# Loading the block-sum input of an attention kernel as one transfer of 128 rows, or as four of 24 rows, one per head

## The chip, the cores and the metric

The kernel runs on one core of a Trainium2 chip. The metric is the device time of one execution in microseconds (us); lower is better. Six names recur: PE is TensorE (matmuls, and PEld its weight loads), DVE is VectorE, ACT is ScalarE, POOL is GpSimd, and SP is the engine that here only issues transfers. "SPq" in a profile line is SP's stream of transfer issues, "POOLq" that of POOL.

## The reference

The inputs are q, k and v of shape (4, 8, 768, 64) in float32, and the weights of a small mixture of attention experts. Cut to what matters:

```
# stage 1, per batch b and head h (S = 768, D = 64, 24 blocks of 32 tokens)
k_sum = k.reshape(B, H, 24, 32, D).max(axis=3)
v_sum = v.reshape(B, H, 24, 32, D).mean(axis=3)
scores_all = concat([where(|i - j| < 16, scale * q @ k.T, -1e9),
                     scale * q @ k_sum.T + log(32)])
x = softmax(scores_all) @ concat([v, v_sum])
# stage 2, per batch: x (768 x 512) goes through 4 causal attention experts (64 wide),
# each token's output is the softmax-weighted sum over its two best experts
```

The change is about how v is brought in for `v_sum`, the mean of v over each block of 32 tokens.

## The kernel before, in words

Batches b run over 0 to 3. In stage 1 the 8 heads of a batch are taken as 4 pairs c; two pairs make a group g of 4 heads. Nothing is scheduled at run time. Every piece of work is a named step, and a table written out by hand (`TABLE`) lists all steps in one order, each with the engine that runs it and the buffer slots that it takes. Each engine executes its own steps strictly in that order, so a step that waits holds everything behind it on its engine. The names used below are a step's kind, then b, then c or g, then a part.

The steps that touch the change:

- `dvs`b g (L373, L376) is issued by SP. It loads the v of 4 heads into the buffer `vt` (128 partitions of 2048 float32). Partition 32*j + n holds block n of head j: 32 tokens of 64 values, 8 KB, contiguous in memory. The rows 24 to 31 of each head's 32 partitions are not used by anything later. `vt` has one slot only, so each load waits until the additions on the one before it have read it.
- `tr`b g 0 and 1 (L384) are the additions on POOL that fold 2048 values to 64, in five instructions (1024, 512, 256, 128, 64 wide) over partitions 0 to 119. The last writes `vu`.
- `ds`b c (L181 on POOL or DVE, L179 on ACT) copies the sums from `vu` into rows 96 to 119 of the value buffer `vb`, twelve times over.
- `dv`b c (L312) is SP's load of v for the window, in rows of 256 bytes, into `vb`.
- `av`b c u (L478 on PE) multiplies the softmax weights by `vb`; it needs both `dv` and `ds`.

This tree of loads and additions is used for the groups (1,1), (2,0), (2,1), (3,0) and (3,1); the others sum v by matmuls (L337).

Around them: `dk` and `dq` (L289) are the loads of k and q, issued by POOL, in POOL's order between the additions; `tk` (L409) and `tq` (L435) are the transposes on PE that need them; `pp` (L653), `vp` (L585, L588), `sp` (L677), `es` (L685 on ACT), `dm` (L690 on POOL), `aw` (L701), `tw` (L737) and `op` (L755) are stage 2 of the previous batch; `od` (L766) is SP's store of the output; L503 is a transpose on PE of the stage 1 result.

SP's order around the loads is: dwv, **dvs11**, dv12, dwo, dv13, **dvs20**, dv21, dv20, **dvs30**, dv23, **dvs21**, od02, dv22, od00, **dvs31**, od01, dv30, dv32. In POOL's order, dk200 and dk210 stand ahead of tr200; dq300, dk310, dq210 and dk300 stand between tr201 and tr300; tr310 follows on tr211 and a copy.

A step of kind `dvs` starts after `vt` was set to zero once, at the beginning (`vtz`, L278).

Of the kernel before, what the change touches and what calls it, by code (L numbers as in the profile page):

```python
# [13 lines left out]
B = 4  # L14
H = 8
S = 768
D = 64
# [5 lines left out]
NSUM = 24  # L23
# [146 lines left out]
def make_plan(nc, T, q, k, v, moe_w_gate, moe_wq, moe_wk, moe_wv, moe_wo, out):  # L170
# [3 lines left out]
    def en(e):  # L174
        return getattr(nc, ENG[e])

    def copy(e, dst, src):
        if e == "A":
            nc.scalar.copy(dst, src)  # L179
        else:  # L180
            en(e).tensor_copy(dst, src)  # L181
# [185 lines left out]
    def tree(b, g):  # L367
        t, u = R.buf("vt"), R.buf("vu")

        def load(e):  # L370
            x, vh = T["vt"][t.slot], v[b, 4 * g]
            full = 4 if (b, g) != (B - 1, 1) else 3
            nc.sync.dma_start(out=x[0:32 * full, :],  # L373
                              in_=bass.AP(vh.tensor, vh.offset, [[S * D, full], [32 * D, 32], [1, 32 * D]]))
            if full == 3:
                nc.sync.dma_start(out=x[96:96 + NSUM, :],  # L376
                                  in_=bass.AP(vh.tensor, vh.offset + 3 * S * D, [[32 * D, NSUM], [1, 32 * D]]))
        R.step(f"dvs{b}{g}", {"S": 1.8}, [vtz], [t], load, dma=3.0)
        for i, ws in enumerate(((1024,), (512, 256, 128, 64))):
            def add(e, ws=ws):  # L380
                x = T["vt"][t.slot]
                for w in ws:
                    y = T["vu"][u.slot] if w == 64 else x[:, 0:w]
                    en(e).tensor_tensor(y[0:120], x[0:120, 0:w], x[0:120, w:2 * w], AL.add)  # L384
            R.step(f"tr{b}{g}{i}", {"G": sum(0.13 + w * 0.00218 for w in ws)}, [t],
                   [u] if i else [t], add, keep=[t])
        for c in (2 * g, 2 * g + 1):
            def dsum(e, c=c):
                for h in range(2):
                    j = 32 * (2 * (c % 2) + h)  # L390
                    copy(e, T["vb"][vb[b, c].slot][WIN:KR, 12 * h + 1:12 * h + 13, 0:64],
                         T["vu"][u.slot][j:j + NSUM, :].unsqueeze(1).to_broadcast((NSUM, NQ, 64)))
            R.step(f"ds{b}{c}", {"G": 1.75, "V": 0.95, "A": 1.64}, [u], [vb[b, c]], dsum)
# [517 lines left out]
```

## Time and profile before

| what | value |
|---|---|
| median of 3 runs | 227.06 us (222.6 to 229.35) |
| the profiled execution's own time | 223.95 us |
| its span, first to last instruction | 222.2 us |
| mean granted TensorE clock | 0.879 of full speed |
| busy PE, DVE, ACT, POOL | 159.6, 136.2, 125.4, 91.7 us |
| additions on `vt` (L384), mean of one of the 20 that write `vt` | 1200 ns |
| POOL's wait for `vt` from memory | 41.5 us in 4 waits |
| moved by transfers | 28.27 MB |

The profile is one execution. Its instructions are shown by engine with their line in the kernel, and idle time is put down to what ended it. The time of an execution is 1.75 us above the span in the profiled run. "DMA share" is the mean busy share of the core's 16 transfer engines.

### The profile page before, as it was taken

The page shows a single profiled execution, that of the slowest core. Times are in us where ns is not written, and L with a number is a line of the kernel's source. Part 1 is how long each engine was busy: PE and PEld are TensorE (multiplying, and loading weights), DVE is VectorE, ACT ScalarE, POOL GpSimd, SP SyncE. Part 2 cuts the span into 40 slices and gives each one's busy share as a digit, 9 for nine tenths or more (in the row PEclk, how much of TensorE's full clock was granted, in tenths as well). Part 3 has the DMA queues.
Part 4 walks back from the last instruction along what each step waited for, and adds up shares of the span by engine and source line. Part 5 has one row for each costly group of instructions (what it writes and reads, how often), then busy time and mean ns, then how long its engine had stood idle before and what let it go on. Part 6 is the DMA issues. An engine that isn't in the chain of part 4 may idle for free.

```text
span 222.2 us, 6444 instructions
## 1 busy us (share of the span) xinstructions
PE 159.6 (72%) x2796; PEld 119.2 (54%) x2796; DVE 136.2 (61%) x251; ACT 125.4 (56%) x158; POOL 91.7 (41%) x149
## 2 busy tenths in 40 slices
PE   0283986599689964989504994399509999999860
PEld 0262875487587752665302683386406688765520
DVE  1779379568958894289602772476045888756740
ACT  8472576377558881468602695027504577578840
POOL 7439255502934807863067404800492242004200
PEclk9996799969969998899955899569955999999997
DMA  5999999932938756699626932492296450011335
GB/s 70 231 206 214 201 198 224 139 78 71 176 77 95 120 107 120 111 141 167 112 48 138 183 102 78 137 221 77 77 239 144 118 85 4 3 43 55 136 132 209
DMA packets 49939, 28.27 MB, mean 127 GB/s; under 512 B 38783, under 2 KB 45951, under 8 KB 49279
## 3 DMA queue, kind: packets, MB, share of 16 engines
q1 hardware_dynamic: 42455, 21.56, 46.4%
q0 software_dynamic: 7456, 6.29, 20.1%
q8 instruction: 22, 0.36, 0.8%
q14 instruction: 6, 0.05, 0.1%
HBM read 27.85 MB, written 6.29 MB: 154 GB/s over the span
## 4 chain that ended last, share of the span: by engine, by line
DMA 37%; PE 30%; POOL 13%; DVE 10%; issue 6%; ACT 2%; SPq 0%; POOLq 0%; ACTq 0%; DVEq 0%
DMA vt<-in_v_dram 35%; POOL vt L384 11%; PE ps L478 6%; PE ps L653 5%; PE ps L503 2%; PE ps L337 2%; PE ps L585 2%; PE ps L677 2%; PE ps L755 2%; PE ps L435 2%; DMA kn<-in_k_dram 2%; DVE ks L419 2%; PE ps L409 2%; DVE vb L246 2%; PE ps L701 2%
## 5 line engine op out<-in xcount | busy, mean ns | idle before, releaser
L685 ACT ACTIVATE a<-ps 128x1024 f16<-128x1024 f32 (+1 forms) x48 | 42.0, 916 | 33.1 <-PE ps L677 19.3
L384 POOL TENSOR_TENSOR vt<-vt 120x1024 f32<-120x1024 f32 (+3 forms) x20 | 24.0, 1200 | 42.6 <-DMA vt<-in_v_dram 41.5
L690 POOL TENSOR_SCALAR_AFFINE_SELECT a<-a 128x256 f16<-128x256 f16 x48 | 18.6, 407 | 42.8 <-ACT a L685 32.7
L478 PE MATMUL ps<-vb,aT 120*64 120x65 f32 x768 | 30.9, 244 | 7.2 <-issue 6.8
L468 ACT ACTIVATE aT<-ps 120x768 f32<-120x768 f32 x32 | 25.4, 816 | 18.6 <-PE ps L461 17.9
L478 PEld LDWEIGHTS ps<-vb,aT 120*64 120x64 f32 x768 | 28.5, 157 | 9.7 <-issue 8.5
L677 PE MATMUL ps<-qk,qk 64*128 64x512 f16 (+3 forms) x128 | 16.2, 330 | 11.4 <-DVE v L181 10.7
L653 PE MATMUL ps<-hi,wqk 128*128 128x384 f16 x128 | 24.0, 340 | 0.0
L435 PE MATMUL ps<-id,qn 128*64 128x128 f16 x192 | 10.2, 265 | 19.0 <-DMA qn<-in_q_dram 14.8
L419 DVE TENSOR_REDUCE ks<-ps 128x24 f16<-128x768 f16 x16 | 14.9, 952 | 9.3 <-PE ps L409 7.5
L435 PEld LDWEIGHTS <-qn 128*64 128x64 f16 x192 | 8.1, 138 | 20.8 <-DMA qn<-in_q_dram 15.4
L409 PE MATMUL ps<-id,kn 96*64 96x96 f16 (+1 forms) x256 | 9.8, 234 | 11.8 <-DMA kn<-in_k_dram 10.1
L653 PEld LDWEIGHTS <-wqk 128*128 128x128 f16 x128 | 12.4, 101 | 9.3 <-issue 2.3
L514 DVE TENSOR_TENSOR lo<-ps,hi 128x768 f16<-128x768 f32 x16 | 15.1, 955 | 2.2 <-ACT hi L179 1.9
L493 DVE TENSOR_TENSOR x<-ps,rec 128x768 f32<-128x768 f32 x16 | 15.3, 957 | 0.7 <-DVE rec L489 0.2
L409 PEld LDWEIGHTS <-kn 96*64 96x64 f16 (+1 forms) x256 | 8.1, 129 | 14.1 <-issue 8.8
L179 ACT COPY kw<-ps 128x1152 f16<-128x1152 f16 x10 | 11.2, 1120 | 7.3 <-DVE ks L419 6.4
L585 PE MATMUL ps<-wvg,hi 128*128 128x264 f16 x96 | 14.8, 287 | 0.6 <-DVE lgp L181 0.6
L179 ACT COPY qT<-ps 128x768 f16<-128x768 f16 x11 | 8.6, 804 | 11.2 <-PE ps L435 11.2
L503 PE MATMUL ps<-id,x 128*128 128x128 f32 x96 | 14.3, 290 | 0.5 <-DVE ks L419 0.5
L181 DVE COPY vb<-vu 24x768 f32<-24x768 f32 x6 | 4.8, 802 | 15.8 <-POOL vu L384 15.7
L677 PEld LDWEIGHTS <-qk 64*128 64x128 f16 x128 | 5.0, 97 | 16.4 <-issue 14.2
(96 smaller groups left out, 311.7 us busy)
## 6 DMA issues: line engine op xcount, KB each, us to landing
out_dram<-ob SPq DMA_DIRECT2D x11, 512.0 KB, 5.1
vt<-in_v_dram SPq DMA_DIRECT2D x4, 1024.0 KB
vb<-in_v_dram SPq DMA_DIRECT2D x7, 576.0 KB, 14.2
vb<-in_v_dram SPq DMA_DIRECT2D x7, 400.0 KB, 15.5
kn<-in_k_dram POOLq DMA_DIRECT2D x7, 384.0 KB, 13.1
qn<-in_q_dram POOLq DMA_DIRECT2D x7, 384.0 KB, 13.1
vt<-in_v_dram SPq DMA_DIRECT2D x1, 768.0 KB
vb<-in_v_dram SPq DMA_DIRECT2D x1, 552.0 KB
```

Source lines behind the costliest of these rows:

```text
L179: nc.scalar.copy(dst, src)
L384: en(e).tensor_tensor(y[0:120], x[0:120, 0:w], x[0:120, w:2 * w], AL.add)
L409: nc.tensor.transpose(pbank16(kp)[64 * hp:64 * hp + 64, o:o + n], src[0:n, hh + hp, 64 * s:64 * s + 64], id16w(n, c0))
L419: nc.vector.tensor_reduce(T["ks"][ks.slot], view(pbank16(kp), PE0, [[4, NSUM], [96, 8], [1, 4]]), AX.XY, AL.max)
L435: nc.tensor.transpose(pbank16(qp)[64 * hp:64 * hp + 64, 128 * s:128 * s + 128], src[:, hh + hp, 64 * s:64 * s + 64], id16w(128))
L468: nc.scalar.activation(T["aT"][aT.slot][0:KR], pbank(sc, 2)[0:KR, :, 0:384], AF.Exp, scale=SCALE)
L478: nc.tensor.matmul(pbank(av, 2)[o:o + 64, u, 65 * (2 * (t // 2) + hp):65 * (2 * (t // 2) + hp) + 65], a[0:KR, hp, 64 * t:64 * t + 64], T[" ...
L503: nc.tensor.transpose(pbank(xp, 2)[:, t // 3, 128 * (t % 3):128 * (t % 3) + 128], T["x32"][x32.slot][:, 128 * t:128 * t + 128], T["id32"])
L585: nc.tensor.matmul(p[:, i, 0:264], hi_(ch)[:, cols], T["wvg"][:, ch, :], start=(ch == 0), stop=False, skip_group_check=True)
L653: nc.tensor.matmul(pbank(pp, 2)[:, u, 0:384], T["wqk"][:, cc, ch, j, :], hi_(ch)[:, 384 * u:384 * u + 384], start=(ch == 0), stop=(ch == N ...
L677: nc.tensor.matmul(pbank(sp, 2)[:, ep, c0:c0 + w], T["qk"][qk[1].slot][r, 128 * tj:128 * tj + 128], T["qk"][qk[0].slot][r, n0:n0 + w], sta ...
L685: nc.scalar.activation(a2v(u), pbank(sp, 2)[:, :, 0:ln], AF.Exp, scale=SCALE / (XS * XS))
```

## The change

The single transfer of 128 rows, from a source described as 4 heads by 32 rows by 2048 values, becomes four transfers of 24 rows by 2048 values, one per head, in the order of heads 0, 2, 1, 3. The group (3,1), which was loaded as 96 rows and then 24 (the last head has no rows behind its 24), is loaded in the same way. The rows 24 to 31 of each head's partitions keep the zeros that `vtz` put there.

```
 def load(e):
-    x, vh = T["vt"][t.slot], v[b, 4 * g]
-    full = 4 if (b, g) != (B - 1, 1) else 3
-    nc.sync.dma_start(out=x[0:32 * full, :],
-                      in_=bass.AP(vh.tensor, vh.offset, [[S * D, full], [32 * D, 32], [1, 32 * D]]))
-    if full == 3:
-        nc.sync.dma_start(out=x[96:96 + NSUM, :],
-                          in_=bass.AP(vh.tensor, vh.offset + 3 * S * D, [[32 * D, NSUM], [1, 32 * D]]))
+    for j in (0, 2, 1, 3):
+        nc.sync.dma_start(out=T["vt"][t.slot][32 * j:32 * j + NSUM, :],
+                          in_=v[b, 4 * g + j].rearrange("(n s) d -> n (s d)", s=32))
```

The order of all other instructions on each engine is the same in both programs. SP issues 20 tree transfers in place of 6. Each transfer on SP counts its completion on one of eight semaphores, taken in turn, and waits until the transfer that last used the same one has landed; 14 more transfers shift this turn for all that follow.

## The prediction

> **What bounds the kernel now.** I read the chain of waits first, since it says what ended last. Its shares, from the page:
>
> ```profile
> DMA 37%; PE 30%; POOL 13%; DVE 10%; issue 6%; ACT 2%; SPq 0%; POOLq 0%; ACTq 0%; DVEq 0%
> ```
>
> 35 of the 37 points of DMA are loads of `vt`. The list of waits (who waited for whom, us in total, times, longest) has as its first line:
>
> ```profile
> POOL vt L384 <- DMA vt<-in_v_dram: 41.5, 4, 14.5
> ```
>
> PE is the busiest engine (159.6 us of 222.2) but only 30% of the chain: PE waits for the loads. The same chain in order of time, for the middle of the span (start us, us, what):
>
> ```profile
> 62.90 21.64 DMA vt<-in_v_dram
> ...
> 84.67 2.34 POOL vt L384
> ...
> 90.37 22.50 DMA vt<-in_v_dram
> ...
> 112.95 2.35 POOL vt L384
> ...
> 118.37 17.94 DMA vt<-in_v_dram
> ...
> 136.39 2.35 POOL vt L384
> ...
> 142.68 15.80 DMA vt<-in_v_dram
> ```
>
> From 62.9 to 164 us the kernel is a ring of one buffer: load, five additions (57.32 to 62.88, or 5.5 us), next load. Four loads take 21.64 + 22.50 + 17.94 + 15.80 = 77.9 us. The fifth, at 34.6, is over before POOL comes to it.
>
> Why does 1 MB take 20 us? Two stretches, with busy times of the engines, granted clock, DMA share and GB/s last:
>
> ```profile
> 113.20:119.20 6.00, 0.00 (x0) 0.00 (x0) 0.00 (x0) 0.00 (x0) 5.62 (x6) 0.50 0.31 48
> 150.00:158.00 8.00, 8.00 (x71) 5.54 (x70) 3.85 (x5) 5.89 (x9) 0.00 (x0) 1.00 0.21 75
> ```
>
> From 150 to 158 hardly anything moves but the 96-row part of the last load. Share 0.21 of 16 engines is a little over three, and the source has an outer dimension of three heads. The packets that the trace records agree: three rows of 8 KB are in flight there, and four (mean 3.7 to 4.0) in each of the other loads, whose source has four heads. So each of four engines carries 32 rows of 0.40 to 0.59 us, 13 to 19 us, while twelve have none. The first stretch shows the second harm: `vt` has landed, and 0.31 of the engines still move 48 GB/s. These are the q and k loads that POOL issued between 95 and 102: their shares on the burdened engines queued behind the rows of `vt`.
>
> What PE loses is read from its order of time (start us, us, engine, line, count, idle before and what ended it):
>
> ```profile
> 86.24 0.54 PE L409 MATMUL ps<-id,kn 98*64 98x98 f16 x16 [4.67 <-DMA kn<-in_k_dram]
> ...
> 87.29 4.16 PE L653 MATMUL ps<-hi,wqk 128*128 128x384 f16 x16
> ...
> 119.46 0.85 PE L435 MATMUL ps<-id,qn 128*64 128x128 f16 x12 [10.86 <-DMA qn<-in_q_dram]
> ...
> 121.82 1.91 PE L755 MATMUL ps<-wo,wT 128*128 128x512 f16 x4
> ...
> 142.48 3.27 PE L478 MATMUL ps<-vb,aT 120*64 120x65 f32 x48 [6.46 <-issue]
> ...
> 166.58 0.61 PE L677 MATMUL ps<-qk,qk 64*128 64x512 f16 x2 [7.90 <-DVE v L181]
> ```
>
> These are gaps A, B, C and D. A and B end with a k and a q load. C is PE's weight load waiting for ds23, and D waits for DVE's v221, which stands behind ds32: both follow on additions that waited for `vt`. After each gap the clock is low (0.50 to 0.73 in stretches of 6 to 10 us around them) and the work slow: sixteen matmuls of L653 take 4.16 us after A, 2.60 later in the chain.
>
> **The change part by part.** *The load.* Unused rows go: 96 are moved in place of 128. The price of a 24-row transfer is in the trace once, the second part of the last load, issued at 142.68 in 0.48 us. Beside the three-row stream, seven to eight more rows are in flight from 143.9 to 144.8, and by 145.2 it is back to three or four: 2.5 us from issue to landing. Four issues cost 0.81 + 2 x 0.53 us before the last (0.81 and 0.48 with its gap are the two issues at 141.82 and 142.68), and the last lands 2.5 us on: 4.4 us. The upper bound takes the dearest row, 0.59 us, and seven in flight: 96 / 7 x 0.59 = 8.1 us, with 0.9 ahead of the first row 9.0 us. I take 4.4 for the load by itself, and 9.0 for what must be covered.
>
> [...]
>
> *Is it covered?* dvs20 is issued at 62.9 and lands by 72; POOL has masks, copies and two k issues until 76.9. dvs30 is issued as tr201 ends and lands by 9 us later; POOL has dm, copies and four q and k issues for 12.7 us (90.0 to 102.7). dvs21 follows tr301 by 0.4 us; POOL has 9.1 us of other work (118.35 to 127.45). dvs31 has the least cover: 2.3 us of ds22 after tr211, so POOL waits 2 to 7 us; but tr210 itself now starts 8.9 us sooner against PE, and D's consumer stands 22 us on. So the wait does not reach PE. If that cover were gone, at most 7 us would show.
>
> *What is recovered.* Gaps: 4.67 + 10.86 + 6.46 + 7.90 = 29.9 us. Slow restarts, against the same groups at full clock elsewhere in the trace: after A 1.6 (L653); after B 2.3 (L755 1.91 against 0.97; L435 0.85 against 0.53; L737 0.3; L677 0.7); after C 2.1 (L478 3.27 against 1.55; L455 and L461 0.35); after D 1.5 (L435 and L409 0.3 each, L585 0.9). Together 7.4.
>
> *What is given back.* First, other engines run on after PE has stopped, and PE may now wait for them: DVE 2.1 us at A, ACT 1.05 at B, 1.4 at C, 1.1 at D. Bounds 0 and 5.7; I take 5.7, since from 165 to 203, where nothing of `vt` is in the way, PE is busy 36.4 of 38.0 us but follows close on DVE and ACT. Second, q and k. The page gives their queue 20.1% of 16 engines' span for 16 loads' worth of 384 KB: 2.8 us an engine each. The fastest q load landed in 6.1 us. At A dk200 has 8.5 us (73.1 to 81.6): lateness 0 to 4.7. At B dq210 is third of its group, issued at 96.8 and wanted at 108.6: three times 2.8 from 95.4 is 104, but dv23 and `vt` are ahead of them, so lateness 0 to 10.9. I take 0.5 and 1.5, near the lower ends, as the burdened engines were the reason.
>
> *Added waits.* The three more issues delay what SP has behind them (dv12, dv21, od02, od01) by 1.6 us each; no PE gap is put down to any of these, so I cost it at nothing (1.6 us once, if dv21 were waited for). By the turn of semaphores the second and third part of dvs21 wait for dv21 and dv20. SP was held 22.3 us over those two issues at 63.7; with short loads it is not, and they land some 20 us ahead of dvs21. If they did not, od02, dv22 and dvs31 would be late behind it, a few us, within the cover of C.
>
> The sum: span 222.2 - 29.9 - 7.4 + 5.7 + 2.0 = 192.6, and with the 1.75 us around the span 194.3 us. That is made against the profiled execution (223.95), which stands 3.1 below the median of 227.06; I do not add that.
>
> **Rivals.**
>
> *All of it is recovered.* Nothing given back: 222.2 - 37.3 + 1.75 = 186.7 us. For it: PE holds clock 1.00 and 10.0 of 10 us busy from 174 to 194. Against: A and B need loads to land in time.
>
> *q and k take the place of `vt`.* If these land as late as now, A and B stay, and only C and D go: 222.2 - 14.4 - 3.6 + 2.5 + 1.75 = 208.5 us. For it: the middle moves the same bytes in some 75 us that took 108. Against: the first 35 us run at around 200 GB/s, the middle at 113 to 130.
>
> *No wider than now.* If the parts follow each other four rows at a time, only the unused quarter goes: 0.25 x 62.1 = 15.5 us of the first three loads, less 11 more issues of 0.53 us: 223.95 - 9.7 = 214.3 us. Against: seven or more rows were in flight at 144.
>
> *Slower: the parts go narrower.* If a 24-row transfer ran on two engines and all four on the same two, each would carry 48 rows against 32 now, and the four loads grow by half: 223.95 + 38.9 = 262.9 us. It decides from fewer than three rows in flight. For it: the lone 192 KB sample ran beside another stream. Against: eleven rows were in flight.
>
> **How the numbers follow.** My forecast, 188 to 201: 0.62. All recovered: 0.14. q and k: 0.13. No wider, or a semaphore wait that eats most: 0.07. Narrower: 0.04. The range for 8 in 10 runs from just under the full recovery, 185, to the q and k case, 208; beyond lie part of the first and the last two. A measurement of this kernel tells about 2% from no change. Faster by over 2% holds the first three and most of the fourth, 0.93; the same 0.03; slower 0.04.
>
> **What would show it.** `vt` should leave the chain, with PE its largest share; a load should take 4 to 9 us; POOL's wait for `vt` should fall from 41.5 us to under 8, most of it before tr310; the four PE gaps should shrink to 1 or 2 us each and the mean clock rise above 0.93. q and k should land in about 10 us. I am wrong if gaps at L409 or L435 remain, if ACT and DVE make up more than 6 us, or if the 24-row loads still take over 12 us.

## The result, and the profile after

The changed kernel takes 190.0 us (median of 4 runs, 186.69 to 193.28) where the kernel before took 225.56 us beside it. The ratio is 0.840, with a 95% interval of 0.829 to 0.851; run again later, 0.836 (0.825 to 0.847). Predicted were 194.3 us and a range of 185 to 208. The profiled execution took 193.28 us, its span is 191.6 us; that one, not the median, is to be set against the sum of the prediction. Some runs of either kernel lie a few per cent above its fastest; the ratios leave these out, and where too few others remain (e5, e7, e11) only medians are given.

The chain that ended last, from the page, by engine and by line:

```profile
PE 63%; DVE 20%; issue 7%; DMA 4%; ACT 3%; POOL 1%; DVEq 0%; POOLq 0%; ACTq 0%
PE ps L474 13%; PE ps L649 10%; PE ps L499 6%; PE ps L431 4%; PE ps L751 4%; PE ps L337 4%; PE ps L697 4%; PE ps L673 4%; PE ps L581 4%; DMA qn<-in_q_dram 4%; PE ps L451 3%; PE ps L457 3%; PE ps L405 3%; DVE vb L181 2%; DVE wav L723 2%
```

`vt` is gone from it (35% before), and PE leads with 63% (30% before). All lines behind the load now read 4 lower: L478 became L474, and so on. The list of waits has one entry of POOL for `vt`, and the page shows q and k landing sooner (last number, median us; 13.1 for both before):

```profile
POOL vt L380 <- DMA vt<-in_v_dram: 6.3, 1, 6.3
```

```profile
kn<-in_k_dram POOLq DMA_DIRECT2D x7, 384.0 KB, 7.4
qn<-in_q_dram POOLq DMA_DIRECT2D x7, 384.0 KB, 9.1
```

PE in order of time, where the four gaps were and where new ones are (idle before and what ended it in brackets):

```profile
84.21 2.77 PE L649 MATMUL ps<-hi,wqk 128*128 128x384 f16 x16
...
105.61 0.39 PE L673 MATMUL ps<-qk,qk 64*128 64x512 f16 x2 [1.67 <-DVE wav L723]
...
116.55 0.85 PE L431 MATMUL ps<-id,qn 128*64 128x128 f16 x12 [2.54 <-issue]
...
128.31 0.28 PE L457 MATMUL ps<-qT,kw 64*128 64x64 f16 x7
129.31 0.26 PE L457 MATMUL ps<-qT,kw 64*128 64x64 f16 x5 [0.73 <-issue]
...
138.24 0.60 PE L673 MATMUL ps<-qk,qk 64*128 64x512 f16 x4
```

Gap A is gone and L649 runs in 2.77 us (4.16 before). Of B 1.67 us are left, now a wait for DVE. C and D are gone, but ahead of L431 stands a gap of 2.54 us that was not there. The packets that the trace records for `vt` show the load itself: a median of 12 rows in flight, 4.7 to 6.1 us from the first row to the last for the last four loads, 14.5 to 20.4 before.

The same places of the program on both clocks tell what each gap gave (us from the start, both profiles):

| place | before | after | gained since the place above |
|---|---|---|---|
| first addition on `vt` | 57.32 | 59.34 | -2.0 |
| end of sixteen L653/L649 after gap A | 91.45 | 86.98 | 6.5 |
| four L677/L673 after gap B | 123.67 | 107.24 | 12.0 |
| six L737/L733 after gap C | 149.55 | 129.51 | 3.6 |
| twelve L435/L431 after gap D | 167.11 | 138.77 | 8.3 |
| end | 222.2 | 191.6 | 2.3 |

### The profile page after: what moved, and what is told of

It is laid out like the page before. It is cut to its first block, busy times and chain, and to the rows that moved or that the text cites. A ratio compares the mean times of both kernels' runs of the same rounds, so it can differ in the third digit from the quotient of the medians.

```text
span 191.6 us, 6464 instructions
## 1 busy us (share of the span) xinstructions
PE 155.5 (81%) x2796; PEld 118.0 (62%) x2796; DVE 137.0 (71%) x251; ACT 125.0 (65%) x158; POOL 91.0 (47%) x149
## 3 DMA queue, kind: packets, MB, share of 16 engines
q0 software_dynamic: 7456, 6.29, 21.4%
## 4 chain that ended last, share of the span: by engine, by line
PE 63%; DVE 20%; issue 7%; DMA 4%; ACT 3%; POOL 1%; DVEq 0%; POOLq 0%; ACTq 0%
PE ps L474 13%; PE ps L649 10%; PE ps L499 6%; PE ps L431 4%; PE ps L751 4%; PE ps L337 4%; PE ps L697 4%; PE ps L673 4%; PE ps L581 4%; DMA qn<-in_q_dram 4%; PE ps L451 3%; PE ps L457 3%; PE ps L405 3%; DVE vb L181 2%; DVE wav L723 2%
## 5 line engine op out<-in xcount | busy, mean ns | idle before, releaser
L681 ACT ACTIVATE a<-ps 128x1024 f16<-128x1024 f32 (+1 forms) x48 | 42.0, 916 | 13.2 <-PE ps L673 10.6
L686 POOL TENSOR_SCALAR_AFFINE_SELECT a<-a 128x256 f16<-128x256 f16 x48 | 18.8, 412 | 47.3 <-ACT a L681 37.3
L464 ACT ACTIVATE aT<-ps 120x768 f32<-120x768 f32 x32 | 25.3, 816 | 12.5 <-PE ps L457 11.8
L474 PE MATMUL ps<-vb,aT 120*64 120x65 f32 x768 | 28.4, 234 | 0.3 <-DVE vs L181 0.3
L474 PEld LDWEIGHTS ps<-vb,aT 120*64 120x64 f32 x768 | 26.2, 148 | 2.6 <-issue 1.6
L649 PE MATMUL ps<-hi,wqk 128*128 128x384 f16 x128 | 22.7, 326 | 0.0
L431 PE MATMUL ps<-id,qn 128*64 128x128 f16 x192 | 9.7, 253 | 11.6 <-DMA qn<-in_q_dram 4.0
L673 PE MATMUL ps<-qk,qk 64*128 64x512 f16 (+3 forms) x128 | 14.9, 307 | 4.8 <-DVE v L181 2.8
L649 PEld LDWEIGHTS <-wqk 128*128 128x128 f16 x128 | 12.0, 98 | 8.2 <-issue 0.6
L510 DVE TENSOR_TENSOR lo<-ps,hi 128x768 f16<-128x768 f32 x16 | 15.1, 954 | 2.5 <-ACT hi L179 2.3
L431 PEld LDWEIGHTS <-qn 128*64 128x64 f16 x192 | 7.6, 131 | 13.5 <-issue 9.1
L499 PE MATMUL ps<-id,x 128*128 128x128 f32 x96 | 15.7, 307 | 0.0
L457 PE MATMUL ps<-qT,kw 64*128 64x64 f16 x384 | 12.3, 198 | 3.6 <-issue 3.6
L581 PE MATMUL ps<-wvg,hi 128*128 128x264 f16 x96 | 13.9, 275 | 0.2 <-DVE lgp L181 0.2
L697 PE MATMUL ps<-v,a 128*128 128x65 f16 x336 | 13.0, 200 | 0.6 <-ACT wT L179 0.6
L697 PEld LDWEIGHTS <-a 128*128 128x128 f16 x336 | 12.2, 101 | 2.1 <-issue 1.4
```

The lines of the kernel that those rows point to most:

```text
L431: nc.tensor.transpose(pbank16(qp)[64 * hp:64 * hp + 64, 128 * s:128 * s + 128], src[:, hh + hp, 64 * s:64 * s + 64], id16w(128))
L464: nc.scalar.activation(T["aT"][aT.slot][0:KR], pbank(sc, 2)[0:KR, :, 0:384], AF.Exp, scale=SCALE)
L474: nc.tensor.matmul(pbank(av, 2)[o:o + 64, u, 65 * (2 * (t // 2) + hp):65 * (2 * (t // 2) + hp) + 65], a[0:KR, hp, 64 * t:64 * t + 64], T[" ...
L499: nc.tensor.transpose(pbank(xp, 2)[:, t // 3, 128 * (t % 3):128 * (t % 3) + 128], T["x32"][x32.slot][:, 128 * t:128 * t + 128], T["id32"])
L581: nc.tensor.matmul(p[:, i, 0:264], hi_(ch)[:, cols], T["wvg"][:, ch, :], start=(ch == 0), stop=False, skip_group_check=True)
L649: nc.tensor.matmul(pbank(pp, 2)[:, u, 0:384], T["wqk"][:, cc, ch, j, :], hi_(ch)[:, 384 * u:384 * u + 384], start=(ch == 0), stop=(ch == N ...
```

## The experiments

The prediction said that the load was slow because four transfer engines carried it. The change does three things together: it spreads the rows, leaves a quarter of them out, and splits the load. Theory W (rows per engine), U (unused rows) and S (the split) were set against each other first. Each diff shows the lines of the load in `tree` that matter, against the changed kernel unless it says otherwise. "Rows of 0.40 us" means that one 8 KB row takes that long on the mean of a load. All times are medians; e1 to e4 ran beside a before of 226.37 us, e5 to e8 beside 224.52, e9 to e12 beside 227.48.

**e1: one transfer of 128 rows, spread wide.**

```
-for j in (0, 2, 1, 3): ...
+vh = v[b, 4 * g]
+o = vh.offset - (32 * 32 * D if (b, g) == (B - 1, 1) else 0)
+nc.sync.dma_start(out=T["vt"][t.slot],
+                  in_=bass.AP(vh.tensor, o, [[32 * D, 128], [1, 32 * D]]))
```

> One transfer of 128 rows again, all its bytes and one issue as before, but its source is 128 rows that follow each other in memory, so it is not described as 4 heads by 32 rows. The blocks land in the wrong rows (from the second head on they are shifted, and for the last group the 128 rows end at the end of v). Theory W (width: what costs is how many rows of 8 KB each transfer engine carries, 32 on four engines before): the rows spread as in a tile of 128 rows, a load lands in 4 to 9 us and the kernel takes 186 to 194 us. Theory S (the split into four transfers is what helps, more of them being under way at once): as before, 220 to 228 us. Theory U (the unused quarter of the rows is what cost): as before, 220 to 228 us.

Measured: 191.88 us, ratio 0.849 (0.819 to 0.878). Some sixteen rows in flight, 3.5 to 4.8 us for the load. S and U fall as causes of the whole: neither the split nor the unused rows is needed for the gain.

**e2: four transfers of 32 rows.**

```
-in_=v[b, 4 * g + j].rearrange("(n s) d -> n (s d)", s=32)
+in_=bass.AP(vh.tensor, vh.offset, [[32 * D, n], [1, 32 * D]])   # n = 32; 24 for the last head
```

> Four transfers, one per head, in the order 0, 2, 1, 3, but of 32 rows (24 for the very last head), so the unused rows are loaded too: the bytes of before in the split of after. Theory W: 8 rows an engine if each transfer spreads over 16, so 186 to 194 us. Theory S: the same, 186 to 194 us. Theory U: the gain goes, 215 to 228 us.

Measured: 188.11 us, ratio 0.837 (0.817 to 0.856), not to be told from the changed kernel. Once the load is wide, the unused rows cost nothing that can be measured (ratio 0.837, and 0.840 without them).

**e3 and e4: four transfers of 24 rows, on four engines and on two.**

```
+vh = v[b, 4 * g]
-in_=v[b, 4 * g + j].rearrange("(n s) d -> n (s d)", s=32)
+in_=bass.AP(vh.tensor, vh.offset + 6 * j * 32 * D, [[S * D, 4], [32 * D, 6], [1, 32 * D]])       # e3
+in_=bass.AP(vh.tensor, vh.offset + (j // 2 * 2 * S + j % 2 * 384) * D,
+            [[S * D, 2], [32 * D, 12], [1, 32 * D]])                                             # e4
```

> Four transfers of 24 rows as in the changed kernel, the same bytes, the same order of issues and waits, but each transfer's source is described as 4 heads by 6 rows, so that its outermost dimension is four as it was before. All 96 rows are moved once, into the wrong places. Theory W: four rows in flight, 24 rows an engine, 10 to 14 us and the issues for a load against 16 to 22 before and 4 to 9 after: 203 to 214 us. Theory S: as after, 186 to 194 us. Theory U: as after, 186 to 194 us.

> As the kernel of four transfers with an outermost dimension of four, but with two: each source is 2 heads by 12 rows. All 96 rows are moved once, into the wrong places. This is the rival on the slow side of the prediction, made on purpose. Theory W: two rows in flight, 48 rows an engine, 19 to 28 us a load: 235 to 263 us, slower than before. Theories S and U: 186 to 194 us.

Measured: e3 196.39 us, ratio 0.877 (0.861 to 0.892); e4 229.65 us, ratio 1.024 (0.994 to 1.053). POOL's wait for `vt`, from the lists of waits of e3 and then of e4:

```profile
POOL vt L382 <- DMA vt<-in_v_dram: 16.3, 2, 9.7
```

```profile
POOL vt L382 <- DMA vt<-in_v_dram: 58.3, 5, 16.4
```

And a stretch of e4 by busy times, clock, DMA share and GB/s, in which little but `vt` moves; 0.14 of 16 engines is little over two:

```profile
130.00:139.00 9.00, 5.16 (x124) 4.27 (x124) 3.19 (x5) 5.40 (x8) 0.00 (x0) 1.00 0.14 49
```

The median of rows in flight is four in e3 and two in e4, so the shape of the source does set the width. But the sizes that W gave failed. e3 is 7 us faster than the near end of what W gave it, and with four engines still takes 30 us less than the kernel before. Its loads last 9.6 to 10.7 us. Two things go together: 24 rows an engine instead of 32, and rows of 0.37 to 0.44 us instead of 0.40 to 0.59. e4 too is below W's range: 48 rows, but of 0.34 to 0.40 us. So the next runs take rows per engine and the split apart.

**e5 and e6: 24 rows an engine in one transfer, 32 in four.**

```
+in_=bass.AP(vh.tensor, vh.offset, [[23 * 32 * D, 4], [32 * D, NSUM], [1, 32 * D]])     # e5, out: partitions 0 to 95
+in_=bass.AP(vh.tensor, vh.offset + r * 32 * D, [[S * D, 4], [32 * D, 8], [1, 32 * D]]) # e6, r = 8 * j (16 for the very last head); out: 32 rows at 32 * j
```

> One transfer of 96 rows into partitions 0 to 95, its source described as four runs of 24 rows, each run starting 23 rows after the last (so that they don't join into one run of 96; three rows are read twice, and the blocks land in the wrong places). One issue as before, four rows in flight as before, but 24 rows an engine instead of 32. The run of four transfers of 24 rows on four engines took 196.4 us, where 203 to 214 were expected. Theory N (the load's length is rows per engine times the time of a row, and the kernel sees only what sticks out beyond some 9 to 11 us of cover): loads of 10 to 14 us, 194 to 205 us. Theory P (the split itself did most there, and a single transfer on four engines keeps the slow rows of 0.56 to 0.59 us): 14 us a load and 203 to 214 us.

> Four transfers of 32 rows, each source 4 heads by 8 rows: the bytes and the 32 rows an engine of before, four rows in flight, but in four transfers. All 128 rows are moved (for the very last group some twice), into the wrong places. Theory N with the rows of 0.37 to 0.44 us seen in the run of four transfers on four engines: 12 to 14 us a load, 197 to 207 us. With the rows of before (0.40 to 0.59 us): 14 to 20 us a load and 216 to 228 us. Theory U (the unused quarter of the rows cost most of the gain once the load is narrow): 216 to 228 us.

Measured: e5 198.0 us; e6 206.43 us, ratio 0.922 (0.915 to 0.929). The waits of e6:

```profile
POOL vt L383 <- DMA vt<-in_v_dram: 27.2, 4, 12.5
```

Theory N's times hold for both (194 to 205 and 197 to 207 us), its loads nearly: those of e5 last 9.4 to 10.8 us, those of e6 12.5 to 15.7. With 24 rows on four engines one transfer does nearly what four do (198.0 against 196.4). But e6 moves the bytes of before, over four engines as before, and is 18 us faster: its rows take 0.36 to 0.46 us in place of 0.40 to 0.59. Two things differ, the split into four transfers and the rows that move at the same time, and e6 does not say which of them makes the rows quicker.

**e7: the kernel before with two slots for `vt`.**

```
-SLOTS = dict(... vt=1, ...)        dvs20,S,0  dvs21,S,0
+SLOTS = dict(... vt=2, ...)        dvs20,S,1  dvs21,S,1
```

> The kernel before, with its narrow single transfer, but two slots for vt in place of one, so that a load waits for the additions of the load before the last and not of the last. Theory R (what cost was the ring of one buffer; the four burdened engines hurt nothing else): the loads are ready when POOL comes, 186 to 196 us. Theory H (the burdened engines hold up q, k and the other loads of v as well): gaps of PE at the k and q transposes stay, and the loads of vt follow each other closely on the same four engines: 200 to 215 us.

Measured: 212.39 us, some 12 us of the 36. The ring is not enough of a cause. The last four loads still take 15.1 to 18.8 us each, POOL still waits for them, and PE for q:

```profile
POOL vt L384 <- DMA vt<-in_v_dram: 26.8, 3, 12.3
```

```profile
107.67 0.85 PE L435 MATMUL ps<-id,qn 128*64 128x128 f16 x12 [7.36 <-DMA qn<-in_q_dram]
```

A second slot lets a load be issued early, but SP's issue of dvs21 at 81.30 (118.37 before) was itself held for 22.42 us, and the first row of that load moved at 107.5.

**e8: the order 0, 1, 2, 3.**

```
-for j in (0, 2, 1, 3):
+for j in range(4):
```

> The changed kernel with the four transfers in the order of heads 0, 1, 2, 3 instead of 0, 2, 1, 3. The additions wait for all four. Every theory so far: no difference that can be told, 185 to 194 us. A theory that the order of the heads matters (neighbouring heads slow each other): loads longer by 1 us or more and POOL's last wait for vt longer, 190 to 197 us.

Measured: 189.35 us, ratio 0.848 (0.840 to 0.855); loads of 4.6 to 5.5 us. The order does nothing that shows.

**e9 and e10: why rows were slow.** Both are one transfer on four engines, against the kernel before.

```
+in_=bass.AP(vh.tensor, o, [[S * D, 4], [32 * D, 30], [1, 32 * D]])            # e9, out: partitions 0 to 119; o: v of the group's first head, for the last group moved back by 6 rows
+in_=bass.AP(vh.tensor, o, [[33 * 32 * D, 4], [32 * D, 32], [1, 32 * D]])      # e10, out: all 128; o as in e9, moved back by 35 rows
```

> One transfer, 4 heads by 30 rows into partitions 0 to 119: what each of the four engines reads is as before (heads 48 rows of 4 KB, or 24 of 8 KB, apart), but the four places that are written at the same time are 30 partitions apart instead of 32. The blocks land in the wrong places. The four transfers of 32 rows on four engines had rows of 0.37 to 0.46 us and took 206.4 us, the kernel before has 0.40 to 0.59 us and took 224.5, with the same bytes, engines and reads; what differs is where the rows go. Theory D (four rows written 32 partitions apart at the same time slow each other): rows of 0.36 to 0.46 us, loads of 11 to 14 us, 198 to 207 us. Theory T (only the other traffic that a long load meets makes its rows slow): rows as before, loads of 12.5 to 18.5 us, 212 to 224 us. [...]

> One transfer of 4 runs by 32 rows into all 128 partitions as before, but the runs start 33 rows apart in v instead of 24, so that reads that are made at the same time lie elsewhere in memory; the writes are as before. The blocks are the wrong ones. Theory D (the places written): as before, rows of 0.40 to 0.59 us, 220 to 229 us. Theory M (the places read at the same time, 24 rows of 8 KB apart, slow each other): rows of 0.36 to 0.46 us, loads of 12 to 15 us, 203 to 211 us.

Measured: e9 214.24 us, ratio 0.943 (0.926 to 0.960), rows of 0.42 to 0.51 us; e10 229.06 us, ratio 1.012 (0.999 to 1.025), rows of 0.42 to 0.63 us. In e9's expectation, "heads 48 rows of 4 KB, or 24 of 8 KB, apart" is the same distance told twice. e10 rules out theory M: other reads, same slow rows. e9 is inconclusive: its time and its loads (14.1 to 16.7 us) are where T put them, its rows fit T and overlap with D. It is also a weak test, since 30 partitions apart is close to 32. So that the places written slow the rows is not shown. T is not the whole either: the last section has slow rows with no other transfer under way.

**e11 and e12: two slots in the changed kernel, and the changed kernel beside it.** The edit in e11 is e7's, and e12 has none.

> The changed kernel with two slots for vt, so that dvs31 can be issued before the additions on dvs21's data are done. POOL's last wait for vt (6.3 us in the profile after) should go. Theory C (that wait is covered, as the prediction says: PE does not wait for what follows it): 187 to 192 us, within 1% of the changed kernel run beside it. Theory L (it shows later, through POOL or the gap of PE near 127 us): 3 to 5 us less than the changed kernel beside it.

> The changed kernel once more, as the measure for the one with two slots on the same chip: 186 to 193 us, and loads of vt of 4.5 to 7.5 us with twelve rows in flight.

Measured: 191.4 and 190.25 us; the fastest runs are 187.08 and 187.09. POOL's wait falls to 2.0 us (5.7 in e12), and the time does not follow:

```profile
POOL vt L380 <- DMA vt<-in_v_dram: 2.0, 1, 2.0
```

Theory C holds, as far as runs that spread over 187 to 195 us can tell: the wait that is left is covered. No version beats the changed kernel by more than its spread.

Put together, in the order of the load's length (first row to last, the last four loads; read from the packets that the traces record):

| kernel | rows an engine | in flight | load, us | POOL's wait, us | time, us |
|---|---|---|---|---|---|
| e1 | 8 | 16 | 3.5 to 4.8 | 4.5 | 191.9 |
| after | 8 | 12 | 4.7 to 6.1 | 6.3 | 190.0 |
| e2 | 8 | 16 | 4.7 to 5.9 | 5.0 | 188.1 |
| e3 | 24 | 4 | 9.6 to 10.7 | 16.3 | 196.4 |
| e5 | 24 | 4 | 9.4 to 10.8 | 16.4 | 198.0 |
| e6 | 32 | 4 | 12.5 to 15.7 | 27.2 | 206.4 |
| e9 | 30 | 4 | 14.1 to 16.7 | 33.5 | 214.2 |
| before | 32 | 4, last 3 | 14.5 to 20.4 | 41.5 | 225.6 |
| e10 | 32 | 4 | 15.5 to 21.4 | 47.5 | 229.1 |
| e4 | 48 | 2 | 16.7 to 21.7 | 58.3 | 229.7 |

With one slot for `vt`, the time follows the length of the load, whatever makes it. From after to e3 the four loads grow by 19 us together (5.2 to 10.1 us each on the mean), and the kernel by 6: most of that is covered. From e3 on it is not: e6 has 14 us more of loads and takes 10 us more, before has 29 more and takes 29 more, e4 39 and 33.

## Why the prediction was right, and where it was not

**The bound.** Right. The four loads of `vt` set the middle of the kernel, and PE does once they are short: 63% of the chain.

**The width.** Right, and shown: sources with an outermost dimension of 2, 4, 24 and 32 or 128 had some two, four, twelve and sixteen rows in flight. (In the kernel before the mean is 3.5 to 3.8 rows for the loads from four heads, a little under the 3.7 to 4.0 of the prediction.) A single transfer into 128 partitions ties with the four when it spreads (e1, 191.9 us), and takes 225.6 us when its source holds it to four engines (before).

**But the width is not the whole cause.** The prediction put the length of the load down to four engines carrying 32 rows. e3 and e5 keep four engines and are already 27 to 30 us faster, so most of the gain did not need the spread. The step that failed is "so each of four engines carries 32 rows of 0.40 to 0.59 us": the 0.59 was taken as the price of a row, where rows of the same size took 0.36 to 0.46 us on four engines in e3, e5 and e6. What makes them quicker stays open. And because most of a load of some 10 us is covered, the last step from four engines to twelve buys only 6 us.

**The price of the new load.** 4.4 us was too low, 9.0 a fair bound. From the first issue at 64.92 the last row ended at 70.9, so 6.0 us; the last four loads took 5.6 to 7.0 us in this way. The issues were cheaper than said, 1.53 us for four, the rows dearer: 0.54 to 0.58 us with twelve in flight.

**The cover.** Right. Only tr310 waits, 6.3 us; "2 to 7" was forecast, and e11 takes the wait away without effect. q and k land in 7.4 and 9.1 us, "about 10" in the text.

**The terms.** The sum was right to a us (191.6 against 192.6 for the span), in part by luck: the profiled execution is the slowest of its four, and the other three took 186.69 to 191.6 us, 2.7 to 7.6 us less than the forecast 194.3. Nor were all its terms right. A: 3.7 net forecast, 6.5 measured; DVE's 2.1 us and k's 0.5 were not given back. B: 10.6 and 12.0; 1.67 us are left as a wait for DVE, where 1.05 for ACT was forecast, and q's 1.5 were not given back. C: 7.2 and 3.6; here the give-back was mis-sized, 1.4 said, 5.0 by difference. PE has new gaps of 2.54 and 0.73 us, and after the first of them the granted clock is low again (0.52 from 117.3 to 123). D: 8.3 and 8.3. Two differences that the forecast did not name cancel: the first 57 us are 2.0 us longer, the end 2.3 us shorter. The same kernel in e12 shows how far one execution can be trusted here: it comes to the first addition at 53.4, so 3.9 us sooner than before and not later, and gains 6.5, 10.8, 4.1, 6.8 and 1.1 us over the same places. The stretch ahead of the first addition is not the change's, A and C are as above, and B and D are good to some 1.5 us.

**What the new gap at C is** was not settled. The prediction would be wrong, it said, if gaps at L409 or L435 remained. One stands at L431, which is L435 after the change, but it does not end with the landing of q. The profile puts it down to "issue", which is a wait for nothing that it shows. The second one cuts a group of twelve matmuls into seven and five. The trace records a transfer of instructions, 16 KB, that starts inside the first gap (114.3 us) and one 2.2 us ahead of the second (126.4), and the gaps return in e1 (2.02 and 2.00 us), e2 (2.20 and 2.37 us), e8 (1.24 and 4.00 us) and e12 (2.06 and 2.35 us). The low clock after the first does not always: in e2 it was 1.00 in the 6.5 us from the end of that gap. That code arriving late is their cause is an inference; no run took it away.

**The rivals.** "Narrower" is e4. Its point of decision held: two rows in flight are no faster than before, four are. Its price did not: 262.9 us against 229.7, since it scaled the slow rows. "No wider than now" was priced at 214.3 us; e3 is that rival, and took 196.4. "q and k take the place" did not happen. "All of it is recovered", 186.7 us, is where the fastest runs lie (186.69 and 187.09); the median is 3 us above it. The mean clock, forecast above 0.93, was 0.927 in the profile after, 0.951 to 0.973 in the other three executions and 0.936 in the profile of e12.

## What to carry to other kernels

Look at how many packets of a large transfer are in flight, not only at its bytes: in these runs a DMA share that stayed near 2/16, 3/16 or 4/16 while little but the load moved (0.14, 0.21, 0.28) went with an outermost dimension of two, three or four. Here 32 rows a head, of which 8 were not needed, kept the source from joining into one run of rows and held 1 MB to four engines. And compare the length of the load with the work that covers it: the gain is what sticks out, so the first cut of a load may bring nearly everything (27 to 30 us in e3 and e5), and a later one, however clever, nothing (e11, 191.4 us beside 190.25).

## What the runs showed of the hardware that was not expected

The time of one 8 KB row is not fixed. Three stretches in which `vt` moves on four engines, two of the kernel before and then one of e6, with clock, DMA share and GB/s at the end. In the first nothing but `vt` moves, in the second little else, in the third q or k loads add about a third of the transfer time:

```profile
72.00:74.00 2.00, 2.00 (x63) 1.80 (x63) 1.86 (x7) 1.46 (x3) 1.90 (x4) 1.00 0.26 66
128.00:134.00 6.00, 5.50 (x166) 4.83 (x167) 4.71 (x10) 5.87 (x7) 0.00 (x0) 1.00 0.28 95
```

```profile
68.00:72.00 4.00, 3.95 (x93) 3.15 (x92) 3.79 (x9) 3.37 (x5) 3.78 (x6) 1.00 0.37 109
```

The kernel before, on four engines in both and at nearly the same share, moves 66 GB/s in one load and 95 in another; its rows take 0.52 and 0.33 us on the mean. In e6 they take 0.33 us, though POOL is nearly always busy there, as it is in the first stretch. In e7, whose transfers are those of before, rows take 0.37 to 0.52 us on the mean of the last four loads. Reads made elsewhere (e10) do not cure it. In the three kernels with wide loads the time of a row went together with where the rows are written: 0.54 to 0.58 us with twelve in flight in the changed kernel, each transfer into 24 partitions, 0.52 to 0.54 us in e2, where each transfer of sixteen goes into 32 partitions, beside 0.37 to 0.45 us in e1, where sixteen go to all 128. Places written alone do not explain the kernel before: its fast load (0.33 us) and its slow one (0.52 us) go to the same partitions. e9 does not decide, and this stays open.

A load on few engines also holds up what is issued after it on SP: two issues (dv21 and dv20) took 22.3 us from 63.7 before and 5.05 us from 66.6 after. The hold shortens with the load in the other runs too: 21.24 us in e4, 11.66 in e6, 8.76 in e3, 4.39 in e1.
